# Decode attention with a gated MLP: TensorE's work on a quad of heads becomes a hardware loop, with semaphores set by hand

## The chip, the cores and the metric

The kernel runs on one core of a Trainium2 chip. The time is the device time of one execution, in microseconds (us). Its parts run side by side on that core's engines: TensorE (PE, with its weight loads listed apart as PEld), VectorE (DVE), ScalarE (ACT), GpSimd (POOL) and SyncE (SP). SP computes nothing here; it issues the large transfers from device memory to SBUF. An engine takes its instructions in program order, and a wait holds back all that stands behind it on the same engine.

## The reference

One token per batch row (B = 2, model width D = 576) goes through two branches, and a gate mixes the results. All of it is float32.

```python
g = _sigmoid((x * gate_w).sum(-1, keepdims=True))
# branch A: attention with a cache; H = 32 heads, Sk = 4096 positions, Dh = 128
q = (x @ wq).reshape(B, Sq, H, Dh).transpose(0, 2, 1, 3)
scores = jnp.einsum("bhqd,bhkd->bhqk", q, k_cache) * (Dh ** -0.5)
p = _softmax(scores, axis=-1)
o = jnp.einsum("bhqk,bhkd->bhqd", p, v_cache)
a = o.transpose(0, 2, 1, 3).reshape(B, Sq, H * Dh) @ wo
# branch B: MLP with F = 4608
h = _gelu(jnp.einsum("bsd,df->bsf", x, w1) + b1)
b = jnp.einsum("bsf,fd->bsd", h, w2) + b2
return g * a + (1 - g) * b
```

Nearly all the data are the two caches: 2 x 32 x 4096 x 128 float32 each for K and for V.

## The kernel before

**Tiles.** Four heads of one batch row make a quad; there are 16 quads, i = 0 to 15. The K rows of a quad, K(i), fill one slot of SBUF: 128 partitions x 16384 float32, 8192 KB, 32 partitions to a head. So do its V rows, V(i). There are three such slots. K alternates between slots 0 and 1, and V(i) goes through slot 2, except the last: V(15) goes into slot 0, where K(14) was.

**Start.** `wq` and `w1` are loaded into the same slots, TensorE makes q (line 170, in PSUM, spread to all partitions) and the MLP's hidden row (line 186), and VectorE and ScalarE apply the activation.

**A quad**, in the loop of line 294:

- `qk(i)`: VectorE multiplies K(i) by q in place (line 230) and sums over Dh (line 231) into the scores `st`; lines 232 to 234 find the maximum of each group of 32 partitions. ScalarE takes the exponential of each head (line 237) into `p`, with the sums in `rs`.
- `av(i)`: TensorE multiplies `p` with V(i), 32 matmuls into one bank of PSUM (line 245, called the products below); ScalarE copies that bank to SBUF (line 249, `avs`).
- `combine(i)`: five small matmuls (lines 258 and 262) add `avs` and `rs` into the bank `oall`, where the results of all quads gather. In the program it stands after `qk(i + 1)`.

`p`, `avs`, `rs`, `st` and the bank of the products exist twice, and quads take turns.

**Order of the transfers.** SP issues K(i + 2) once line 231 has read K(i) out of its slot, and V(i + 1) once the products of quad i have read V(i) out of slot 2. V(15) is the exception: its slot is free when line 231 of quad 14 is done. Behind the quads come the rows of `w2` and `wo` (line 273): 28 rows of `w2` into slot 2, after the products of quad 14; 14 rows of `wo` into slot 1, after line 231 of quad 15; the other 8 rows of `w2` and the last 5 of `wo` into slot 0, after V(15) has been read.

**End.** VectorE scales the gathered outputs into `oT` (lines 323 to 331), TensorE multiplies `hg` by `w2` and `oT` by `wo` as the rows land (lines 284 and 356), and the sum goes out (line 364).

The order on every engine is that of the program text, under a framework that sets all waits from what an instruction reads and writes.

Of the kernel before, what the change touches and what calls it, by code (L numbers as in the profile page):

```python
# [1 line left out]

# [6 lines left out]
F32 = mybir.dt.float32  # L9
AF = mybir.ActivationFunctionType  # L10
ALU = mybir.AluOpType
AX = mybir.AxisListType
P = 128


@with_exitstack
def kernel(
    ctx: ExitStack,
    tc: tile.TileContext,
    x: bass.AP,  # L20
    k_cache: bass.AP,
    v_cache: bass.AP,
    wq: bass.AP,
    wo: bass.AP,
    w1: bass.AP,
    b1: bass.AP,
    w2: bass.AP,
    b2: bass.AP,
    gate_w: bass.AP,
    out: bass.AP,  # L30
):
# [6 lines left out]
    G = H // HQ  # L38
# [15 lines left out]

    cp = ctx.enter_context(tc.tile_pool(name="cp", bufs=1))
    pp = ctx.enter_context(tc.tile_pool(name="pp", bufs=1, space=bass.MemoryType.PSUM))
    ctx.enter_context(tc.manual_schedule())

    def sb(name, *shape):
        return cp.tile(list(shape), F32, tag=name, name=name)  # L60

    slots = [sb(f"slot{i}", P, SLOT) for i in range(3)]
    dma = nc.sync.dma_start
# [6 lines left out]
    nc.scalar.dma_start(xg[:B], x.rearrange("b s d -> (b s) d"))  # L70
    nc.scalar.dma_start(xg[B:B + 1], gate_w[None, :])
    nc.scalar.dma_start(b1T, b1.rearrange("(p r) -> p r", r=FR))
    nc.scalar.dma_start(b2r, b2[None, :])


    qrow = wq[:XR].rearrange("(p r) n -> p (r n)", r=NX)
    hrow1 = w1[:XR].rearrange("(p r) n -> p (r n)", r=NX)
    wqh = slots[1][:, SLOT - WQ // 2:]
    dma(slots[0], qrow)
    dma(wqh, wq[XR:].rearrange("q (e n) -> (q e) n", e=2))  # L80
    FA = 3
    dma(slots[1][:, :FA * F], hrow1[:, :FA * F])
    dma(slots[2][:, :F], hrow1[:, FA * F:])
    w1h = slots[2][:, F:F + F // 2]
    dma(w1h, w1[XR:].rearrange("q (e n) -> (q e) n", e=2))
# [3 lines left out]
    def load_quad(src, i, s):  # L89
        g, b = divmod(i, B)  # L90
        dma(slots[s], src[b, g * HQ:(g + 1) * HQ].rearrange("h (p r) d -> (h p) (r d)", p=HP))
# [3 lines left out]
    make_identity(nc, ident)  # L95
    pt = []
    for j in range(2):
        t = sb(f"p{j}", P, R * HQ + 32)
        nc.vector.memset(t, 0.0)
        pt.append(t)  # L100
    e16 = sb("e16", P, 16)
    nc.vector.tensor_reduce(e16, ident.rearrange("p (j c) -> p j c", j=4)[:, :, :16].rearrange("p j c -> p c j"),
                            AX.X, ALU.add)
    hm = sb("hm", P, HQ)
    nc.vector.tensor_reduce(hm, ident.rearrange("p (h i) -> p h i", h=HQ), AX.X, ALU.add)
    dm = sb("dm", P, DQ)
    nc.vector.tensor_reduce(dm, ident.rearrange("p (a q) -> p q a", q=DQ), AX.X, ALU.add)
    sel = sb("sel", P, 2, 4, 32)
    hsel = sb("hsel", P, 2, 32)
    nc.vector.memset(sel, 0.0)  # L110
    nc.vector.memset(hsel, 0.0)
    for gp in range(2):
        c = slice(16 * gp, 16 * gp + 16)
        for rr in range(4):
            nc.vector.tensor_copy(
                sel[:, gp, rr, c].rearrange("p (h q) -> p h q", q=DQ),
                e16[:, 4 * rr:4 * rr + 4].unsqueeze(2).to_broadcast([P, HQ, DQ]),
            )
        nc.vector.tensor_copy(
            hsel[:, gp, c].rearrange("p (h q) -> p h q", q=DQ), hm.unsqueeze(2).to_broadcast([P, HQ, DQ])  # L120
        )


    qps = [[pp.tile([P, 512], F32, tag=f"q{b}{m}", name=f"q{b}{m}") for m in range(2)] for b in range(B)]
    avp = [pp.tile([P, 512], F32, tag=f"av{j}", name=f"av{j}") for j in range(2)]
    oall = pp.tile([P, 512], F32, tag="oall", name="oall")
    misc = pp.tile([P, 512], F32, tag="misc", name="misc")
# [4 lines left out]
    nc.vector.memset(xe, 0.0)  # L132
    for e in range(2):
        nc.vector.tensor_copy(xe[:, e, e::2], xg[:, XR:])  # L134
    NC6 = NX + 2
    xps = misc[:, :4 * NC6].rearrange("p (c k) -> p c k", k=4)
    for c in range(NC6):
        src = xg[:, c:XR:NX] if c < NX else xe[:, c - NX]
        nc.tensor.transpose(xps[:, c, :B + 1], src, ident[:B + 1, :B + 1])
    xT = sb("xT", P, NC6, 32)  # L140
    nc.vector.memset(xT, 0.0)
    nc.vector.tensor_copy(xT[:, :, :B], xps[:, :, :B])
    xq = sb("xq", P, NC6, B)
    nc.vector.tensor_scalar_mul(xq, xps[:, :, :B], SCALE)
    gT = sb("gT", P, NC6)
    nc.vector.tensor_copy(gT, xps[:, :, B])
    zps = misc[:, 64:64 + B]
    for c in range(NX + 1):
        nc.tensor.matmul(zps, gT[:, c:c + 1].to_broadcast([P, P]), xT[:, c, :B], start=(c == 0), stop=(c == NX))
    gb = sb("gb", P, B)  # L150
    g1 = sb("g1", P, B)
    nc.scalar.activation(gb, zps, AF.Exp, scale=-1.0)
    nc.vector.tensor_scalar_add(gb, gb, 1.0)
    nc.vector.reciprocal(gb, gb)
    nc.vector.tensor_scalar(g1, gb, -1.0, 1.0, op0=ALU.mult, op1=ALU.add)
# [3 lines left out]
    nc.vector.memset(g1z, 0.0)  # L159
    for u in range(2):  # L160
        nc.vector.tensor_copy(g1z[:, u, 32 * u:32 * u + B], g1[0:1])
    for u in range(2):
        nc.tensor.matmul(acc, g1z[:, u], b2r[:, u * DW:(u + 1) * DW], start=(u == 0), stop=False, skip_group_check=True)  # L163


    def q_mm(c, t, m, last):
        v = t.rearrange("p (g h d) -> p g h d", h=HQ, d=DH)
        for b in range(B):
            for h in range(HQ):
                nc.tensor.matmul(  # L170
                    qps[b][m][HP * h:HP * (h + 1)], xq[:, c, b:b + 1].to_broadcast([P, HP]), v[:, :, h],
                    start=(c == 0), stop=last, skip_group_check=True,
                )

    for c in range(NX):
        for m in range(2):
            o = c * WQ + m * WQ // 2
            q_mm(c, slots[0][:, o:o + WQ // 2], m, False)
    for e in range(2):
        q_mm(NX + e, wqh, e, True)  # L180


    hps = [avp[0], avp[1], oall]

    def mlp_mm(c, t, j, m, last):
        nc.tensor.matmul(  # L186
            hps[m][32 * j:32 * j + 32, :FC], xT[:, c], t, start=(c == 0), stop=last, skip_group_check=True
        )

    for c in range(NX):  # L190
        t = slots[1][:, c * F:(c + 1) * F] if c < FA else slots[2][:, :F]
        for m in range(3):
            for j in range(4):
                o = j * FJ + m * FC
                mlp_mm(c, t[:, o:o + FC], j, m, False)
    for m in range(3):
        for j in range(4):
            e = j // 2
            o = (j % 2) * FJ + m * FC
            mlp_mm(NX + e, w1h[:, o:o + FC], j, m, True)  # L200

    for m in range(3):
        nc.scalar.copy(hr[:, m * FC:(m + 1) * FC], hps[m][:, :FC])  # L203
# [8 lines left out]
    nc.vector.tensor_mul(gt, gt, hb)  # L212
    nc.scalar.activation(gt, gt, AF.Tanh, scale=0.7978845608028654)
    nc.vector.tensor_scalar(gt, gt, 1.0, 0.5, op0=ALU.add, op1=ALU.mult)
    nc.vector.tensor_mul(gt, gt, hb)
    nc.vector.tensor_mul(hg, gt, g1.unsqueeze(1).to_broadcast([P, FR, B]))


# [174 lines left out]
```

## Time and profile before

| | |
|---|---|
| median of 3 runs | 726.17 us (726.03 to 727.52) |
| the profiled execution | 726.76 us, of which its span is 724.9 us |
| VectorE busy | 572.6 us (79%) |
| TensorE busy | 216.1 us (30%) |
| ScalarE busy | 45.7 us (6%) |
| read from device memory | 308.57 MB, 426 GB/s over the span |

The span goes from the first instruction to the last; the remaining 1.9 us of the profiled execution lie around it. In rows of a timeline the first number is the start in us from the span's start, the second the length in us; `SPq` is SP issuing a transfer, and the length there is only the issuing. A row may merge several instructions (x2). `PE ... x64` are the 32 products of one quad, since each matmul leaves two records. The number in square brackets is how long the engine stood idle before the row, with what ended it.

### The profile page before, as it was taken

Reading aid. Unit: us, or ns where it says so; the run is one execution under the profiler, and the core shown is the slowest. Engines: PE = TensorE matmul, PEld = TensorE weight load, DVE = VectorE, ACT = ScalarE, POOL = GpSimd, SP = SyncE. Lnnn points to the kernel's source line nnn. Section 1 sums busy time; section 2 is a strip of 40 time slices with the busy share of each in tenths; the row PEclk is TensorE's granted clock in tenths of the full one; section 3 lists DMA queues with packets and bytes.
Section 4 is the critical chain, followed back from the end, with each engine's and each line's share of the span. In section 5 each row is a group of like instructions: output and inputs, shape, how many; then the busy total and the mean of one; then the engine's idle time right before and its main releaser. Section 6 shows DMA issues by size and latency. Waiting matters only on the chain.

```text
span 724.9 us, 4058 instructions
## 1 busy us (share of the span) xinstructions
PE 216.1 (30%) x1784; PEld 76.2 (11%) x1784; DVE 572.6 (79%) x127; ACT 45.7 (6%) x150; POOL 0.7 (0%) x6
## 2 busy tenths in 40 slices
PE   1690005050504022140505050504132230505564
PEld 1230002010201001010101010101010010101121
DVE  2003999999999998989899898989898989899000
ACT  0000010101010101010100101010101010100000
POOL 0000000000000000000000000000000000000000
PEclk9996557575666657575757575756657575757789
DMA  9999999999999999999999999999999999999996
GB/s 406 409 461 409 452 412 413 430 438 427 438 427 441 427 438 427 438 431 434 434 434 435 430 438 430 435 434 434 430 438 427 438 428 434 430 438 431 424 413 248
DMA packets 6809, 308.83 MB, mean 426 GB/s; under 512 B 892, under 2 KB 900, under 8 KB 1416
## 3 DMA queue, kind: packets, MB, share of 16 engines
q1 hardware_dynamic: 6632, 308.55, 98.7%
q8 instruction: 14, 0.23, 0.1%
q10 hardware_dynamic: 160, 0.03, 0.0%
q14 instruction: 3, 0.02, 0.0%
HBM read 308.57 MB, written 0.00 MB: 426 GB/s over the span
## 4 chain that ended last, share of the span: by engine, by line
DVE 48%; DMA 48%; PE 3%; issue 0%; SPq 0%; ACTq 0%; DVEq 0%
DMA slot<-in_A_k_cache_dram 33%; DVE st L231 24%; DVE slot L230 24%; DMA slot<-in_A_v_cache_dram 6%; DMA slot<-in_A_wo_dram 6%; DMA slot<-in_B_b_dram 3%; PE q L170 2%; PE av L245 1%; PE misc L163 0%; SPq L273 0%; DVE mx L232 0%; PE q L356 0%; DVE mt L233 0%; DVE nm L234 0%; ACTq L70 0%
## 5 line engine op out<-in xcount | busy, mean ns | idle before, releaser
L230 DVE TENSOR_TENSOR slot<-slot,q 128x16384 f32<-128x16384 f32 x16 | 275.5, 17219 | 44.8 <-DMA slot<-in_A_k_cache_dram 44.7
L245 PE MATMUL av<-slot,p 128*32 128x512 f32 x1024 | 144.8, 729 | 454.7 <-DMA slot<-in_A_v_cache_dram 454.7
L231 DVE TENSOR_REDUCE st<-slot 128x128 f32<-128x16384 f32 x16 | 275.5, 17219 | 1.5
L245 PEld LDWEIGHTS av<-slot,p 128*32 128x32 f32 x1024 | 40.2, 131 | 546.8 <-issue 546.8
L237 ACT ACTIVATE p<-st,nm 32x128 f32<-32x128 f32 x64 | 33.0, 516 | 180.7 <-DVE nm L234 179.4
L249 ACT COPY avs<-av 128x512 f32<-128x512 f32 x16 | 9.4, 586 | 400.8 <-PE av L245 400.8
L207 DVE STREAM_TRANSPOSE slot<-slot 128x1152 f32<-128x1152 f32 x1 | 2.2, 2197 | 40.2 <-ACT slot L203 40.2
L347 DVE COPY avs<-misc 128x288 f32<-128x288 f32 x1 | 0.5, 457 | 32.8 <-PE misc L284 32.8
L258 PE MATMUL oall<-avs,sel 128*32 128x128 f32 x128 | 17.0, 276 | 12.3 <-ACT avs L249 12.3
L170 PE MATMUL q<-slot,xq 128*32 128x512 f32 x160 | 18.7, 630 | 0.0
L258 PEld LDWEIGHTS oall<-avs,sel 128*32 128x32 f32 x128 | 12.7, 109 | 26.9 <-ACT avs L249 26.9
L284 PE MATMUL misc<-slot,hg 128*2 128x288 f32 x144 | 10.5, 453 | 9.5 <-DMA slot<-in_B_w_dram 9.5
L237 ACT ACTIVATION_READ_ACCUMULATOR p<-st,nm 32x1 f32 x64 | 12.5, 196 | 0.0
L323 DVE RECIPROCAL rg<-oall 128x2 f32<-128x2 f32 x1 | 0.2, 171 | 14.8 <-PE oall L262 14.8
L284 PE MATMUL misc<-slot,oT 128*2 128x288 f32 x108 | 7.5, 406 | 6.9 <-DMA slot<-in_A_wo_dram 4.1
L186 PE MATMUL av<-slot,xT 128*32 128x384 f32 x80 | 7.3, 486 | 0.0
L170 PEld LDWEIGHTS q<-slot,xq 128*32 128x32 f32 x160 | 5.0, 117 | 13.6 <-issue 13.6
L134 DVE COPY slot<-slot 3x64 f32<-3x64 f32 x2 | 0.3, 182 | 6.4 <-DMA slot<-in_gate_w_dram 6.4
L163 PE MATMUL misc<-slot 1*128 1x288 f32 x4 | 2.3, 715 | 10.3 <-DMA slot<-in_B_b_dram 10.3
L284 PEld LDWEIGHTS misc<-slot,hg 128*2 128x2 f32 x144 | 3.6, 92 | 16.0 <-DMA slot<-in_B_w_dram 10.2
L232 DVE TENSOR_REDUCE mx<-st 128x1 f32<-128x128 f32 x16 | 4.6, 286 | 0.5
L186 PE MATMUL oall<-slot,xT 128*32 128x384 f32 x40 | 4.1, 486 | 0.0
(58 smaller groups left out, 42.4 us busy)
## 6 DMA issues: line engine op xcount, KB each, us to landing
slot<-in_B_w_dram SPq DMA_DIRECT2D x1, 8064.0 KB, 29.3
slot<-in_B_w_dram SPq DMA_DIRECT2D x1, 6912.0 KB, 41.1
slot<-in_B_w_dram SPq DMA_DIRECT2D x2, 2304.0 KB, 46.1
slot<-in_A_wo_dram SPq DMA_DIRECT2D x1, 4032.0 KB
slot<-in_A_wo_dram SPq DMA_DIRECT2D x1, 1728.0 KB
slot<-in_B_w_dram SPq DMA_DIRECT2D x1, 1152.0 KB
slot<-in_A_wo_dram SPq DMA_DIRECT2D x1, 1152.0 KB, 36.4
slot<-in_A_wo_dram SPq DMA_DIRECT2D x2, 576.0 KB, 38.9
```

The costliest lines, as they stand in the source:

```text
L163: nc.tensor.matmul(acc, g1z[:, u], b2r[:, u * DW:(u + 1) * DW], start=(u == 0), stop=False, skip_group_check=True)
L170: nc.tensor.matmul(qps[b][m][HP * h:HP * (h + 1)], xq[:, c, b:b + 1].to_broadcast([P, HP]), v[:, :, h], start=(c == 0), stop=last, skip_gr ...
L186: nc.tensor.matmul(hps[m][32 * j:32 * j + 32, :FC], xT[:, c], t, start=(c == 0), stop=last, skip_group_check=True)
L207: nc.vector.transpose(ht.rearrange("p (r i) -> p r i", i=32), hr.rearrange("p (i r) -> p r i", r=FR))
L230: nc.vector.tensor_mul(k, k, q.unsqueeze(1).to_broadcast([P, R, DH]))
L231: nc.vector.tensor_reduce(stt[i % 2], k, AX.X, ALU.add)
L232: nc.vector.tensor_reduce(mxt[i % 2], stt[i % 2], AX.X, ALU.max)
L237: nc.scalar.activation(pt[i % 2][a, h:R * HQ:HQ], stt[i % 2][a], AF.Exp, bias=nmt[i % 2][a], accum_out=rst[i % 2][a])
L245: nc.tensor.matmul(avp[i % 2][32 * j:32 * j + 32], pt[i % 2][:, 16 * t:16 * t + 32], v[:, 512 * t:512 * (t + 1)], start=(t < 4), stop=(t > ...
L249: nc.scalar.copy(avt[i % 2], avp[i % 2])
L258: nc.tensor.matmul(oall[a, b * DH:(b + 1) * DH], sel[:, gp, rr], avt[i % 2][:, rr * DH:(rr + 1) * DH], start=first and rr == 0, stop=last ...
L284: nc.tensor.matmul(acc[64 * s + 32 * u:64 * s + 32 * u + B], lhs, wrow[name, r][:, u * DW:(u + 1) * DW], start=False, stop=last, skip_grou ...
```

## The change

The whole program is written in one block in which no framework sets waits. A class `Order` records, for named pieces of data, who wrote and who read them, and puts the semaphore waits in front of an instruction. TensorE's work on quads 0 to 14 is written once, in a hardware loop that runs on TensorE alone (`nc.Fori`, lines 405 to 407), and quad 15 follows as straight code. Inside the loop four semaphores are waited on and set by hand: `exps` (the exponentials are there), `vin` (V has landed; 16 counts to a transfer), `avc` (the copy of the products is there), and towards the others `avd` (products done) and `cmb` (combine done).

Since a loop's body has fixed addresses, `p` (now `pt`), the bank of the products, `avs` and `rs` exist once, and V is counted on one semaphore for all 15 passes. The combine stands right behind the products and its copy. It no longer adds up all quads in one bank: it writes one bank (`cps`) for all 128 partitions, and ScalarE copies the 32 partitions of its quad into the SBUF tile `oS` (line 359). `st`, `nm` and the K slots still come twice. In the start, the matmuls of the second bias stand behind those of q.

```diff
+    def soft(i):
+        j = i % 2
+        o.wait("ACT", o.deps([f"nm{j}", f"st{j}"], ["pt", "rs"]))
         for h in range(HQ):
             a = slice(HP * h, HP * (h + 1))
-            nc.scalar.activation(
-                pt[i % 2][a, h:R * HQ:HQ], stt[i % 2][a], AF.Exp, bias=nmt[i % 2][a], accum_out=rst[i % 2][a]
-            )
...
+            ins = nc.scalar.activation(pt[a, h:R * HQ:HQ], stt[j][a], AF.Exp, bias=nmt[j][a], accum_out=rs[a])
+        ins.then_inc(exps, 1)
+
+    def gather(i):
...
+        nc.scalar.wait_ge(avd, i + 1)
+        nc.scalar.copy(avs, avp).then_inc(avc, 1)
+        a = slice(32 * (g // 2), 32 * (g // 2) + 32)
+        nc.scalar.wait_ge(cmb, i + 1)
+
+        op("ACT", lambda e: e.copy(oS[a, b, g % 2], cps[a, :DH + 1]), r=[f"st{j}", f"nm{j}"], w=[f"oS{i}"])
+
+    def quad_products(e, v):
+        e.wait_ge(exps, 1).then_inc(exps, -1)
+        e.wait_ge(vin, 16).then_inc(vin, -16)
         for t in range(NT):
             j = t % 4
...
+            ins = e.matmul(avp[32 * j:32 * j + 32], pt[:, 16 * t:16 * t + 32], v[:, 512 * t:512 * (t + 1)],
+                           start=(t < 4), stop=(t >= NT - 4))
+        ins.then_inc(avd, 1)
+        e.wait_ge(avc, 1).then_inc(avc, -1)
         for rr in range(4):
...
+            e.matmul(cps[:, :DH], sel[:, rr], avs[:, rr * DH:(rr + 1) * DH],
+                     start=(rr == 0), stop=(rr == 3), skip_group_check=True)
+        e.matmul(cps[:, DH:DH + 1], hsel, rs, start=False, stop=True, skip_group_check=True).then_inc(cmb, 1)
...
     for i in range(NQ):
-        qk(i, i % 2)
+        qk(i)
         if i < NQ - 2:
-            load_quad(k_cache, i + 2, i % 2)
-        elif i == NQ - 2:
-            load_quad(v_cache, N1, i % 2)
-        else:
-            load_rows("wo", 0, WA // 2, N1 % 2, 0)
-        if i > 0:
-            combine(i - 1)
-        av(i, 2 if i < N1 else (NQ - 2) % 2)
-        if i < NQ - 2:
-            load_quad(v_cache, i + 1, 2)
-        elif i == NQ - 2:
-            load_rows("w2", 0, WA, 2, 0)
-    load_rows("w2", WA, FR, 0, 0)
+            k_load(i + 2)
+        soft(i)
+        if i < N1:
+            gather(i)
+            nc.sync.wait_ge(avd, i + 1)
+            if i < NQ - 2:
+                nc.sync.dma_start(slots[2], quad(v_cache, i + 1)).then_inc(vin, 16)
+            else:
+
+                o.wait("SP", o.deps([], ["s0"]))
+                nc.sync.dma_start(slots[0], quad(v_cache, N1)).then_inc(vin, 16)
+    o.wait("PE", o.deps(["sel0", "sel1", "sel2", "sel3", "hsel", "pt"], ["avp", "cps"]))
+    with nc.Fori(0, N1, engines=[PE], head_slot={PE: 0}):
+        quad_products(nc.tensor, slots[2])
+    quad_products(nc.tensor, slots[0])
+    gather(N1)
...
+    load_rows("w2", 0, WA, 2, 0)
+    load_rows("wo", 0, WA // 2, 1, 0, extra=o.deps([], ["s1"]))
+    load_rows("w2", WA, FR, 0, 0, extra=[done(avd, NQ)])
```

On SP, around the last V, before the change (names: `slot0` to `slot2` with a buffer number; the waits in brackets are on transfers, `DMAHW`, and on engines):

```order
L91 DMA slot2_65<-in_A_v_cache_dram 128x16384 [waits DMAHW3_49,PE_49]
L91 DMA slot1_64<-in_A_k_cache_dram 128x16384 [waits DMAHW2_49,DVE_49]
L91 DMA slot2_65<-in_A_v_cache_dram 128x16384 [waits DMAHW5_49,PE_49]
L91 DMA slot0_63<-in_A_v_cache_dram 128x16384 [waits DMAHW4_49,DVE_49]
L273 DMA slot2_65<-in_B_w2_dram 128x16128 [waits DMAHW7_49,PE_49]
L273 DMA slot1_64<-in_A_wo_dram 128x8064 [waits DMAHW6_49,DVE_49]
L273 DMA slot0_63<-in_B_w2_dram 128x4608 [waits DMAHW0_49,PE_49]
```

The same place with the change (`cDVE` counts VectorE's instructions, `avd` the quads whose products are done):

```order
L400 DMA slot2<-in_A_v_cache_dram 128x16384 [waits avd]
L82 DMA slot1<-in_A_k_cache_dram 128x16384 [waits cDVE]
L400 DMA slot2<-in_A_v_cache_dram 128x16384 [waits avd]
L404 DMA slot0<-in_A_v_cache_dram 128x16384 [waits cDVE,avd]
L82 UNCONDITIONAL_BRANCH
L82 DMA slot2<-in_B_w2_dram 128x16128
L82 DMA slot1<-in_A_wo_dram 128x8064 [waits cDVE]
L82 DMA slot0<-in_B_w2_dram 128x4608 [waits avd]
```

The order of the transfers is the same. The row that fills slot 0 with V(15) waited on VectorE alone beside an old transfer, and now waits on `avd` as well, at the value 15; the `w2` row behind it has no wait left.

On TensorE, two quads before the change:

```order
L245 MATMUL av0_109<-slot2_65,p0_81 32x512 [waits DMAHW7_49,Activation_49]
L245 MATMUL av0_109<-slot2_65,p0_81 32x512 x31
L258 MATMUL oall_111<-avs0_310,sel_91 32x128 [waits Activation_49]
L258 MATMUL oall_111<-avs0_310,sel_91 32x128 x3
L262 MATMUL oall_111<-rs0_308,hsel_92 32x1
L245 MATMUL av1_110<-slot2_65,p1_83 32x512 [waits DMAHW1_49,Activation_49]
L245 MATMUL av1_110<-slot2_65,p1_83 32x512 x31
```

The loop with the change, and the first row of quad 15 behind it:

```order
L406 ISA [waits cACT,cDVE]
L406 UNCONDITIONAL_BRANCH
L366 MATMUL bank4<-slot2,pt 32x512 [waits exps,vin]
L366 MATMUL bank4<-slot2,pt 32x512 x31
L371 MATMUL bank5<-avs,sel 128x128 [waits avc]
L371 MATMUL bank5<-avs,sel 128x128 x3
L373 MATMUL bank5<-rs,hsel 128x1
L406 REGISTER_ALU
L406 COMPARE_AND_BRANCH
L366 MATMUL bank4<-slot0,pt 32x512 [waits exps,vin]
```

The products and the combine of a quad stand in the same order as before; what is new between two quads is a register operation and a branch, and the combine's outputs are 128 partitions high where they were 32.

More of the change, by code (lines that the diff above doesn't have):

```diff
@@ L32, with kernel, body @@
+def kernel(tc, *args):
+    with tc.tile_critical():
+        body(tc, *args)
+def body(tc, x, k_cache, v_cache, wq, wo, w1, b1, w2, b2, gate_w, out):
     nc = tc.nc
@@ L173, in q_mm @@
                 )
[L175 to L191, printed above, removed]
+        return ins
```

475 lines of the change are left out of this document (276 added, 199 removed).

## Prediction

> **What bounds the kernel now.** I read the slices of the span first, then the bytes, then three stretches of 39 us.
>
> ```profile
> span 724.9 us, 4058 instructions
> DMA  9999999999999999999999999999999999999996
> HBM read 308.57 MB, written 0.00 MB: 426 GB/s over the span
> 607.00:646.00 39.00, 10.57 (x74) 3.56 (x74) 35.41 (x6) 2.65 (x9) 0.00 (x0) 0.63 1.00 434
> 646.00:685.00 39.00, 20.56 (x148) 7.13 (x148) 23.91 (x8) 3.24 (x10) 0.00 (x0) 0.72 1.00 431
> 685.00:724.00 39.00, 20.05 (x300) 7.11 (x300) 1.72 (x6) 0.00 (x0) 0.00 (x0) 0.91 0.81 344
> ```
>
> In a stretch's row the last three numbers are the TensorE clock, the busy share of the DMA engines and GB/s. The DMA engines are full from the start to the last slice, at 434 GB/s in the steady part; VectorE is busy 35.41 of 39 us, TensorE 10.57. The time is 308.57 MB / 434 GB/s = 711 us, and 14 us of start and end. So one question decides about any edit: does it ever leave the DMA engines without a transfer? For that I read the timeline of the last quads.
>
> ```profile
> 614.88 9.48 PE L245 MATMUL av<-slot,p 128*32 128x512 f32 x64 [28.50 <-DMA slot<-in_A_v_cache_dram]
> 624.42 5.89 SPq L91 DMA_DIRECT2D slot<-in_A_v_cache_dram  x2
> 624.48 0.59 ACT L249 COPY avs<-av 128x512 f32<-128x512 f32 x1 [30.19 <-PE av L245]
> 625.12 1.06 PE L258 MATMUL oall<-avs,sel 128*32 128x128 f32 x8 [0.76 <-ACT avs L249]
> 626.01 0.20 PE L262 MATMUL oall<-rs,hsel 128*32 128x1 f32 x2
> 629.99 0.28 DVE L232 TENSOR_REDUCE mx<-st 128x1 f32<-128x128 f32 x1
> 632.79 0.19 ACT L237 ACTIVATION_READ_ACCUMULATOR p<-st,nm 32x1 f32 x1
> 634.12 17.22 DVE L230 TENSOR_TENSOR slot<-slot,q 128x16384 f32<-128x16384 f32 x1 [3.38 <-DMA slot<-in_A_k_cache_dram]
> 653.58 8.90 PE L245 MATMUL av<-slot,p 128*32 128x512 f32 x64 [27.37 <-DMA slot<-in_A_v_cache_dram]
> 662.54 0.33 SPq L273 DMA_DIRECT2D slot<-in_B_w_dram  x1
> 668.69 0.33 SPq L273 DMA_DIRECT2D slot<-in_A_wo_dram  x1
> 672.94 9.46 PE L245 MATMUL av<-slot,p 128*32 128x512 f32 x64 [8.60 <-DMA slot<-in_A_v_cache_dram]
> 678.12 0.33 SPq L273 DMA_DIRECT2D slot<-in_B_w_dram  x1
> 685.65 0.23 DVE L331 TENSOR_TENSOR oT<-avs,rg 128x64 f32<-128x64 f32 x1
> 691.90 8.41 PE L284 MATMUL misc<-slot,hg 128*2 128x288 f32 x112 [7.65 <-DMA slot<-in_B_w_dram]
> ```
>
> Each row that ends with "<-DMA" dates a landing. K(15) lands at 634.1, V(14) at 653.6, V(15) at 672.9, 28 rows of `w2` at 691.9: 19.4 us apart, back to back. The SP row x2 holds two issues: V(14) at 624.42, when the products of quad 13 end (614.88 + 9.48), and V(15) at about 630.0, when line 231 of quad 14 ends (line 232 follows at 629.99). So V(15) is queued 23.6 us before V(14) has landed. The chain of waits says the same, and that the end hangs on the queue:
>
> ```profile
> 629.98 42.83 DMA slot<-in_A_v_cache_dram
> 680.39 39.87 DMA slot<-in_A_wo_dram
> ...
> 721.01 0.47 PE q L356 x8
> ```
>
> The last piece waits for the last row of `wo`, which lands just before 721.0.
>
> **The change part by part.** *V(15) waits for the products of quad 14: the term that decides.* In the order after the change this transfer waits on `avd` at 15. Those products cannot begin before V(14) has landed, at 653.58, and they end at 662.48. At 653.58 nothing else is queued: the `w2` row stands behind V(15) on SP, and the `wo` row needs line 231 of quad 15 (it went out at 668.69) and stands behind both. The DMA engines run dry. V(15) goes out at 662.54, where the `w2` row went out before (0.06 us behind the products), and starts on an empty queue. How long does an 8192 KB transfer take then? The trace has one, the first transfer of all, of the same shape:
>
> ```profile
> 0.74 0.39 SPq L79 DMA_DIRECT2D slot<-in_A_wq_dram  x1
> slot<-in_A_wq_dram SPq DMA_DIRECT2D x1, 22.1
> ```
>
> It takes 22.1 us from issue to landing, 2.7 more than the 19.4 of one that follows another. V(15) lands at 662.54 + 22.1 = 684.6, where it landed at 629.98 + 42.83 = 672.8: **11.8 us later**. Bounds: with no start-up at all, 662.54 + 19.4 = 681.9, +9.1. Dearest in the trace is a transfer that was issued into a queue about to run dry:
>
> ```profile
> 105.26 0.33 SPq L91 DMA_DIRECT2D slot<-in_A_k_cache_dram  x1
> 109.50 9.58 PE L245 MATMUL av<-slot,p 128*32 128x512 f32 x64 [54.63 <-DMA slot<-in_A_v_cache_dram]
> 148.94 8.64 PE L245 MATMUL av<-slot,p 128*32 128x512 f32 x64 [28.06 <-DMA slot<-in_A_v_cache_dram]
> ```
>
> K(2) goes out at 105.26 and V(1) lands behind it at 148.94, so K(2) at 148.94 - 19.4 = 129.5, 24.3 after its issue; part of that was V(0)'s remainder (landed at 109.50), hence an upper bound: +14.0. I take 22.1, since that transfer also met an empty queue. [...]
>
> *What follows V(15).* The products of quad 15 move from 672.9 to about 684.7 and end at 694. The second part of `w2` waits for them now; before, it went out at 678.12. In the queue then are `w2` (till 691.9 + 11.8 = 703.7) and 14 rows of `wo`, so 9.7 us remain and nothing runs dry again. `oT` was ready at 685.9, 3.5 us after the products; with one more copy of 0.6 us that is about 698, and it is wanted only behind the `w2` rows. So the whole tail moves rigidly, and no later slack takes the 11.8 back: the end waits for arriving rows up to the last.
>
> *The other V loads.* They waited for the products before as well, so nothing is added: V(14) went out at 624.42, with K(15) under way until 634.1, 9.7 us ahead; less the 2.7 of start-up, 7.0 us of cover. Without it each us would cost one us in 14 quads.
>
> *The loop's branch, and waits on TensorE.* They stand between 626.2, where the combine ends, and the next landing; TensorE sits idle 27.4 us there. Cost 0. A few sequencer steps ahead of the first product (two waits instead of one) I put at 0, with 0.2 us as the bound.
>
> *Single `p`, `rs`, `avs`.* The exponentials of quad i + 1 now wait until ScalarE has copied the combine of quad i, because the copy stands ahead of them on ScalarE. That is done at 626.2 + 0.6 (an `avs` copy takes 0.59); line 232 of the next quad starts only at 629.99, the exponentials were ready at 633.0, and the products want them at 653.6. Cost 0, cover 20.6 us. VectorE's next write of the same `st` waits for that copy too; it is line 231 of quad 15, behind line 230 that ends at 651.3. Cost 0. The combine's outputs (1.06 us and 0.20 now) become four times as high, inside the same gap.
>
> *Start and end.* The q matmuls no longer stand behind the second bias, so K(0) may go out earlier; it took 28.82 us from its issue, 6.7 over the 22.1 on an empty queue, so it stood queued behind `w1`: gain 0. The block adds a meeting of the engines before the first transfer and one after the last. The rows for both, K(0) first, then the two meetings that the trace shows:
>
> ```profile
> 41.84 28.82 DMA slot<-in_A_k_cache_dram
> ...
> SPq L379 <- PEq L379: 0.7, 1, 0.7
> SPq L388 <- PEq L388: 0.6, 2, 0.4
> ```
>
> Nothing covers the meetings: bounds 0 and 0.7 + 0.6 = 1.3; I take 0.6. Less code is fetched:
>
> ```profile
> PE 216.1 (30%) x1784; PEld 76.2 (11%) x1784; DVE 572.6 (79%) x127; ACT 45.7 (6%) x150; POOL 0.7 (0%) x6
> ...
> q8 instruction: 14, 0.23, 0.1%
> ```
>
> At most 0.23 MB / 434 GB/s = 0.5 us is to be had there. I take 0.
>
> **Sum:** 11.8 + 0.6 = +12.4 us. The profiled execution would go from 726.76 (span 724.9) to 739.2, the median of 726.17, 0.6 below it, to **738.6**. Own range: 726.0 + 9.1 = 735.1 to 727.5 + 14.0 + 1.3 = 742.8.
>
> **Rivals.** *1. The loop stalls within a pass.* If TensorE had to fetch the loop's code again while the products run, each set of products would grow; from 7.0 us on, V(i + 1) comes late and each further us costs 14 us, and a smaller stall of s us still adds s once, through quad 14. A stall of 3 us gives 741.6, one of 10 us 738.6 + 10 + 3.0 x 14 = 791. For it: the branch is new. Against it: the 14 fetches of 0.23 MB are 16 KB each, and the body is 37 matmuls of the 892 that the program had (1784 records), so it needs no new piece of code in mid-pass unless it lies across a boundary; a fetch at the branch has 27 us. [...]
>
> *2. The transfers catch up: not slower.* Here the queue empties as I say, but what is left then, V(15) with 8.39 MB, `w2` with 10.62 and `wo` with 9.44 (from their shapes), runs faster than before. Short stretches do show more:
>
> ```profile
> 25.00:30.00 5.00, 5.00 (x24) 1.47 (x26) 0.00 (x0) 0.00 (x0) 0.00 (x0) 1.00 0.82 354
> 30.00:35.00 5.00, 5.00 (x52) 1.44 (x48) 0.00 (x0) 0.00 (x0) 0.00 (x0) 1.00 1.17 509
> ```
>
> From 653.6 to the last landing near 721.0 these 28.45 MB take 67.4 us; at 509 GB/s it would be 55.9. That gives 738.6 - 11.5 = 727.1, no change, and it decides from about 500 GB/s. Against it: the neighbour of 509 is 354, and the stretches of 39 us quoted at the start lie at 434 and 431; the peaks are large packets ending in one stretch or the next.
>
> *3. The meetings of the block cost more*, with code to fetch on the way, 3 to 6 us in all instead of 0.6: 741 to 744. It is the same sign, and only the first transfer's start and the rows after the last output tell it.
>
> **How the numbers follow.** My forecast 0.84, rival 1 0.06 (a third of it under 742.8), rival 3 0.05, rival 2 0.05. A difference of 0.2% (1.5 us) is about what a measurement of this kernel can tell from none. The first, second and third of these are slower, 0.95; of rival 2's 0.05 I give 0.03 to no change and 0.02 to faster. The range is the own range, 735.1 to 742.8: it leaves out rival 2, most of rival 1 and half of rival 3, with the edges of the forecast.
>
> **What would show it.** In the profile after: the slices of DMA show a dent near 650 to 665 and nowhere else; V(15) is issued when the products of quad 14 end, and lands 31 us after V(14) instead of 19.4; all rows behind them are 11 to 13 us later, all before 650 within 1 us of their places; the first transfer goes out at 0.7 to 1.5 us. Wrong: products in the loop that last over 10.5 us, landings of V more than 39 us apart in the steady part (rival 1), the last 28.4 MB in under 60 us (rival 2), or a first transfer after 2 us (rival 3).

## The result, and the profile after

The changed kernel takes 738.49 us (median of 6, 737.96 to 739.19) against 726.21 us (median of 6, 725.24 to 727.52) before: a ratio of 1.0167, 95% interval 1.0154 to 1.0180. It is slower by 12.3 us. The forecast was 738.6.

The page of the changed kernel, its span and its slices:

```profile
span 737.4 us, 4073 instructions
...
DMA  9999999999999999999999999999999999939995
GB/s 399 412 443 445 416 419 430 434 434 434 434 431 434 437 434 430 434 437 430 434 430 441 434 430 430 437 430 437 430 437 430 434 430 434 437 153 402 445 415 227
```

One slice stands out: the 36th, 645 to 664 us, with 153 GB/s; the same slice before had 438. The stretches of 12 us around it (the last two numbers: busy share of the DMA engines, GB/s) and the timeline of TensorE and SP show what happens there:

```profile
640.00:652.00 12.00, 0.00 (x0) 0.00 (x0) 11.96 (x2) 0.00 (x0) 0.00 (x0) 0.50 0.77 333
652.00:664.00 12.00, 10.09 (x74) 3.68 (x74) 12.00 (x1) 0.85 (x2) 0.00 (x0) 0.84 0.26 87
664.00:676.00 12.00, 0.00 (x0) 0.00 (x0) 3.93 (x4) 2.06 (x8) 0.00 (x0) 0.59 1.01 437
```

```profile
652.23 8.85 PE L366 MATMUL bank<-slot,pt 128*32 128x512 f32 x64 [27.24 <-PEq L363]
661.13 0.33 SPq L404 DMA_DIRECT2D slot<-in_A_v_cache_dram  x1
661.50 0.43 SPq L82 DMA_DIRECT2D slot<-in_B_w_dram  x1
683.21 8.72 PE L366 MATMUL bank<-slot,pt 128*32 128x512 f32 x64 [20.10 <-PEq L363]
703.24 8.83 PE L454 MATMUL bank<-slot,hg 128*2 128x288 f32 x112 [9.28 <-DMA slot<-in_B_w_dram]
```

V(14) lands at 652.2. Its products run until 661.1, and V(15) is issued 0.05 us later. It lands at 683.2: 22.1 us after its issue, and 31.0 us after V(14). Before, that distance was 19.4 us (653.58 to 672.94). Meanwhile the DMA engines moved 87 GB/s over 12 us. The wait named beside the products is now TensorE's own sequencer (`PEq`), which holds the wait for `vin` (the count that says that V has landed); it is still the landing of V that ends it (the last of the 16 counts of V(15) came at 683.08 us, its products began at 683.21).

The rest of the difference is small, and of both signs. V(14) itself lands 1.4 us earlier than before. The second part of `w2` lands 10.3 us later than before, and yet the output goes out 12.1 us later. The rows for both and for the last rows of `wo`, in the kernel before and then in the change:

```profile
708.51 2.12 PE L284 MATMUL misc<-slot,hg 128*2 128x288 f32 x32 [1.87 <-DMA slot<-in_B_w_dram]
715.46 1.15 PE L284 MATMUL misc<-slot,oT 128*2 128x288 f32 x16 [1.16 <-DMA slot<-in_A_wo_dram]
717.55 1.14 PE L284 MATMUL misc<-slot,oT 128*2 128x288 f32 x12 [0.94 <-DMA slot<-in_A_wo_dram]
721.88 0.65 SPq L364 DMA_DIRECT2D out_dram<-avs  x1
```

```profile
718.80 2.12 PE L454 MATMUL bank<-slot,hg 128*2 128x288 f32 x32 [2.43 <-DMA slot<-in_B_w_dram]
725.74 4.20 PE L454 MATMUL bank<-slot,oT 128*2 128x288 f32 x28 [0.80 <-DMA slot<-in_A_wo_dram]
733.96 0.65 SPq L82 DMA_DIRECT2D out_dram<-pt  x1
```

The TensorE clock of the change in two stretches there (third number from the end):

```profile
721.00:724.00 3.00, 1.04 (x20) 0.49 (x24) 0.00 (x0) 0.00 (x0) 0.00 (x0) 1.00 1.00 422
724.00:727.00 3.00, 2.20 (x24) 0.44 (x20) 0.00 (x0) 0.00 (x0) 0.00 (x0) 0.52 1.00 411
```

28 records (the rows of 16 and 12, one row now) took 1.15 + 1.14 us before, and 4.20 us now. At 724 the granted clock fell to half, just when the last rows came. Four parts make the +12.5 us of the profiled spans: -1.4 at V(14), +11.6 at V(15), +1.8 from there to the output and +0.4 from the output to the end (737.4 - 733.96 against 724.9 - 721.88).

### The profile page after: what moved, and what is told of

The parts are those of the page before. It is cut to its first block, busy times and chain, and to the rows that moved or that the text cites. A ratio compares the mean times of both kernels' runs of the same rounds, so it can differ in the third digit from the quotient of the medians.

```text
span 737.4 us, 4073 instructions
## 1 busy us (share of the span) xinstructions
PE 223.6 (30%) x1784; PEld 79.8 (11%) x1784; DVE 572.7 (78%) x123; ACT 49.6 (7%) x166; POOL 0.7 (0%) x6
## 5 line engine op out<-in xcount | busy, mean ns | idle before, releaser
L336 DVE TENSOR_TENSOR slot<-slot,bank 128x16384 f32<-128x16384 f32 x16 | 275.5, 17218 | 44.9 <-DMA slot<-in_A_k_cache_dram 44.9
L366 PE MATMUL bank<-slot,pt 128*32 128x512 f32 x1024 | 146.1, 735 | 461.4 <-PEq L363 461.4
L366 PEld LDWEIGHTS bank<-slot,pt 128*32 128x32 f32 x1024 | 40.3, 132 | 554.7 <-issue 554.7
L347 ACT ACTIVATE pt<-st,nm 32x128 f32<-32x128 f32 x64 | 33.0, 516 | 153.3 <-DVE nm L340 152.5
L235 PE MATMUL bank<-slot,xq 128*32 128x512 f32 x160 | 19.7, 656 | 8.1 <-DMA slot<-in_A_wq_dram 8.1
L371 PE MATMUL bank<-avs,sel 128*128 128x128 f32 x128 | 18.1, 284 | 12.7 <-PEq L369 12.7
L371 PEld LDWEIGHTS bank<-avs,sel 128*128 128x128 f32 x128 | 15.5, 191 | 26.8 <-issue 26.8
L454 PE MATMUL bank<-slot,hg 128*2 128x288 f32 x144 | 11.0, 466 | 11.7 <-DMA slot<-in_B_w_dram 11.7
L347 ACT ACTIVATION_READ_ACCUMULATOR pt<-st,nm 32x1 f32 x64 | 12.5, 196 | 0.0
L454 PE MATMUL bank<-slot,oT 128*2 128x288 f32 x108 | 9.7, 489 | 3.6 <-DMA slot<-in_A_wo_dram 3.6
L235 PEld LDWEIGHTS bank<-slot,xq 128*32 128x32 f32 x160 | 5.1, 120 | 21.9 <-issue 13.6
L454 PEld LDWEIGHTS bank<-slot,hg 128*2 128x2 f32 x144 | 3.7, 93 | 18.5 <-DMA slot<-in_B_w_dram 12.3
```

Of the source, the lines that this page charges most:

```text
L235: ins = e.matmul(qps[b][m][HP * h:HP * (h + 1)], xq[:, c, b:b + 1].to_broadcast([P, HP]), v[:, :, h], start=(c == 0), stop=last, skip_grou ...
L336: op(V, lambda e: e.tensor_mul(k, k, q.unsqueeze(1).to_broadcast([P, R, DH])), r=["q", s], w=[s])
L347: ins = nc.scalar.activation(pt[a, h:R * HQ:HQ], stt[j][a], AF.Exp, bias=nmt[j][a], accum_out=rs[a])
L366: ins = e.matmul(avp[32 * j:32 * j + 32], pt[:, 16 * t:16 * t + 32], v[:, 512 * t:512 * (t + 1)], start=(t < 4), stop=(t >= NT - 4))
L371: e.matmul(cps[:, :DH], sel[:, rr], avs[:, rr * DH:(rr + 1) * DH], start=(rr == 0), stop=(rr == 3), skip_group_check=True)
L454: ins = e.matmul(acc[64 * s + 32 * u:64 * s + 32 * u + B], lhs[:, r], wrow[name, r][0][:, u * DW:(u + 1) * DW], start=False, stop=r >= hi ...
```

## The experiments

The theory: the price is the dry queue alone, and a transfer that starts on it lands 22 us after its issue. The rivals: the loop or the single buffers cost part of it; a dry queue costs a fixed price, however long it is dry; the transfers make the loss good. The times of the kernel before beside these runs had medians of 725.95 to 726.36 us.

### The last V early, on a semaphore of its own

The wait had a reason: `vin` counts to 16 for each V, so two V loads under way would be counted as one. With a semaphore of its own the last V needs no wait for the products.

```diff
             gather(i)
-            nc.sync.wait_ge(avd, i + 1)
             if i < NQ - 2:
+                nc.sync.wait_ge(avd, i + 1)
                 nc.sync.dma_start(slots[2], quad(v_cache, i + 1)).then_inc(vin, 16)
             else:
                 o.wait("SP", o.deps([], ["s0"]))
-                nc.sync.dma_start(slots[0], quad(v_cache, N1)).then_inc(vin, 16)
+                nc.sync.dma_start(slots[0], quad(v_cache, N1)).then_inc(vlast, 16)
+                nc.sync.wait_ge(avd, i + 1)
...
-    quad_products(nc.tensor, slots[0])
+    quad_products(nc.tensor, slots[0], vlast)
```

> Edit: the last V load is counted on a semaphore of its own and goes out when line 337 of quad 14 is done, without waiting for the products of quad 14; loop, single buffers and all else stay. Theory (the dry queue is the whole cost): V(15) issued near 628.6, landing 19.4 us after V(14) instead of 31.0, time 738.5 - 11.6 = 726.9, within 1 us of the kernel before. Rival A (the loop, the single buffers or the block cost part of it): the dent in DMA is gone, but the time stays 2 us or more above the kernel before, 728.5 to 732. Rival B (the tail's half TensorE clock, 1.8 us in the profile of the change, belongs to the new program and not to the phase of the clock): the last wo products run at half clock here too, and the time is about 728.5.

Measured: 724.80 us (12 executions), 0.9984 of the kernel before (0.9975 to 0.9994). The issue of the last V, the landings of V(14) and V(15), and the stretch that had been empty:

```profile
628.36 0.33 SPq L404 DMA_DIRECT2D slot<-in_A_v_cache_dram  x1
652.02 9.24 PE L367 MATMUL bank<-slot,pt 128*32 128x512 f32 x64 [26.85 <-PEq L364]
671.37 9.80 PE L367 MATMUL bank<-slot,pt 128*32 128x512 f32 x64 [8.07 <-PEq L364]
```

```profile
652.00:664.00 12.00, 10.49 (x74) 3.77 (x74) 12.00 (x1) 0.84 (x2) 0.00 (x0) 0.81 1.01 437
```

V(15) follows V(14) by 19.35 us and the queue stays full. The whole loss is gone with this one wait, so neither the loop nor the single buffers cost anything that can be seen; rival A falls. The sign of rival B is there, but not its time: in this execution too the last rows met half the clock (0.52 from 715 to 718 us), and 12 records took 2.08 us where 1.14 is usual.

```profile
714.41 2.08 PE L455 MATMUL bank<-slot,oT 128*2 128x288 f32 x12 [0.96 <-DMA slot<-in_A_wo_dram]
```

What I had not expected is that the variant is faster than the kernel before, by 1.5 us, and 13.7 us faster than the change, 1 to 2 us more than the dry queue explains.

### The same wait in the kernel before

```diff
-        elif i == NQ - 2:
-            load_quad(v_cache, N1, i % 2)
...
-        av(i, 2 if i < N1 else (NQ - 2) % 2)
+        av(i, 2)
...
         elif i == NQ - 2:
-            load_rows("w2", 0, WA, 2, 0)
-    load_rows("w2", WA, FR, 0, 0)
+            load_quad(v_cache, N1, 2)
+            load_rows("w2", 0, WA, 0, 0)
+    load_rows("w2", WA, FR, 2, 0)
...
```

> Edit on the kernel before: V(15) goes into slot 2 behind V(14), so that it waits for the products of quad 14, and the rows that stood in slot 2 behind it go into slot 0, in the same order; no loop, double buffers as before. Theory: the same dry queue, V(15) lands 31 us after V(14), time 726.2 + 11.7 = 737.9 (737 to 739). Rival A: less than that, by what the loop and the single buffers cost in the change (2 to 6 us less).

Measured: 739.06 us (4 executions, 737.43 to 739.27), ratio 1.0174 (1.0160 to 1.0189), at the upper edge of what was expected.

```profile
653.17 8.49 PE L245 MATMUL av<-slot,p 128*32 128x512 f32 x64 [27.77 <-DMA slot<-in_A_v_cache_dram]
661.72 0.33 SPq L91 DMA_DIRECT2D slot<-in_A_v_cache_dram  x1
683.58 8.65 PE L245 MATMUL av<-slot,p 128*32 128x512 f32 x64 [20.07 <-DMA slot<-in_A_v_cache_dram]
```

The same wait, put into the kernel before with its double buffers and without a loop, costs as much as the whole change: the landing comes 21.9 us after the issue, 30.4 us after V(14).

### How long it is dry: part of the products, and twice

Two variants of the change let V(15) go after the first, or after the sixteenth, of the 32 matmuls; by then the count of V(14) has been taken off `vin`.

```diff
             ins = e.matmul(avp[32 * j:32 * j + 32], pt[:, 16 * t:16 * t + 32], v[:, 512 * t:512 * (t + 1)],
                            start=(t < 4), stop=(t >= NT - 4))
+            if t == 0:          # the other variant: t == 15
+                ins.then_inc(vread, 1)
...
-            nc.sync.wait_ge(avd, i + 1)
             if i < NQ - 2:
+                nc.sync.wait_ge(avd, i + 1)
...
                 o.wait("SP", o.deps([], ["s0"]))
+                nc.sync.wait_ge(vread, i + 1)
                 nc.sync.dma_start(slots[0], quad(v_cache, N1)).then_inc(vin, 16)
+                nc.sync.wait_ge(avd, i + 1)
```

> Edit on the change: V(15) waits only until the first product of quad 14 has been issued and done (V(14) has landed and been counted), not until the last. Theory (time = issue of V(15) + 22.1 us): V(15) is issued about 0.6 to 1.1 us after V(14) lands instead of 8.9, lands about 23 us after it instead of 31.0, and the time is 738.5 - 8 = 730.5 (729.5 to 731.5). A rival by which the dry queue has a fixed price however long it lasts: 736 or more. A rival by which the start-up costs nothing: 727.5.

> Edit on the change: V(15) waits for the first 16 of the 32 matmuls of quad 14, not for all of them. Theory (landing = issue + 22 us): the first half runs at half clock, V(15) is issued 5.5 to 7 us after V(14) lands instead of 8.9 to 9.5, lands 27.5 to 29 us after it, and the time is 735 to 737. Rival (a fixed price): 738.5.

A third lets the `w2` load behind V(15) wait for the products of quad 15, which it need not:

```diff
-    load_rows("w2", 0, WA, 2, 0)
+    load_rows("w2", 0, WA, 2, 0, extra=[done(avd, NQ)])
```

> Edit on the change: the w2 load behind V(15) waits for the products of quad 15 too, though its slot is free, so the queue runs dry a second time. Theory (landing = end of the products + 22 us for about 8 MB): w2 goes out near 692.0, lands near 713.8 instead of 703.2, and the time is 738.5 + 10.6 = 749.1 (748 to 750.5). Rival (a dry stretch is made good in part by the later transfers): under 747.

Issue of V(15) and its landing, in the variant of the first matmul, then in the variant of the sixteenth:

```profile
653.71 0.33 SPq L407 DMA_DIRECT2D slot<-in_A_v_cache_dram  x1
675.79 9.45 PE L367 MATMUL bank<-slot,pt 128*32 128x512 f32 x64 [12.49 <-PEq L364]
```

```profile
658.53 0.33 SPq L407 DMA_DIRECT2D slot<-in_A_v_cache_dram  x1
680.48 8.88 PE L367 MATMUL bank<-slot,pt 128*32 128x512 f32 x64 [16.60 <-PEq L364]
```

In the variant with the second wait, V(15) and then `w2` (the first `wo` rows, which stand behind `w2` on SP and went out at 667.27 in the change, go out at 694.54 here):

```profile
663.03 0.33 SPq L404 DMA_DIRECT2D slot<-in_A_v_cache_dram  x1
684.90 9.21 PE L366 MATMUL bank<-slot,pt 128*32 128x512 f32 x64 [19.89 <-PEq L363]
694.17 0.33 SPq L82 DMA_DIRECT2D slot<-in_B_w_dram  x1
716.45 8.69 PE L454 MATMUL bank<-slot,hg 128*2 128x288 f32 x112 [20.30 <-DMA slot<-in_B_w_dram]
```

| V(15) waits for | issued after V(14) landed | lands after its issue | lands after V(14) | time, median and range, us |
|---|---|---|---|---|
| nothing (own semaphore) | 23.7 before it | | 19.4 | 724.80 (724.22 to 727.69) |
| the first matmul | 2.0 | 22.1 | 24.1 | 731.36 (729.64 to 732.38) |
| the sixteenth | 5.8 | 22.0 | 27.7 | 734.96 (733.90 to 735.22) |
| all (the change) | 8.9 | 22.1 | 31.0 | 738.49 (737.96 to 739.19) |
| all, and `w2` for the products of quad 15 | 9.7 | 21.9, `w2` 22.3 | 31.6 | 750.28 (749.29 to 750.77) |

From the first matmul to the change the issue moves by 6.9 us and the time by 7.1. From the own semaphore to the first matmul the landing moves by 4.7 us; the profiled executions differ by as much (729.64 - 724.76 = 4.9), the medians by 6.6, and the rest is not explained. So, to within some 2 us, there is no fixed price beyond the 2.7 us of start-up (22.1 - 19.4), and nothing is made good later. The expectations held but for edges: the half clock did not last for the whole first half with the sixteenth (it was 0.50 from 640 to 652 us and 0.80 on the mean from 652 to 664, so by an estimate half until about 656.8, 4.1 of the 5.8 us; in the change 0.50 until 655.8 and 1.00 from 655.9 to 661.1), the first matmul's count reached SP 2.0 us after the landing where I had put 0.6 to 1.1, the time with the sixteenth lies just under the 735 expected, and the second dry stretch cost 11.8 us instead of 10.6, since the products of both quads took longer than in the change (V(15) was issued 0.8 us later after V(14), and the products of quad 15 took 9.2 us) and `w2` landed 0.3 us later.

### The loop written out

```diff
-    with nc.Fori(0, N1, engines=[PE], head_slot={PE: 0}):
-        quad_products(nc.tensor, slots[2])
+    for _ in range(N1):
+        quad_products(nc.tensor, slots[2])
```

In the change:

> Edit on the change: the loop over 15 quads is written out as straight code, with the same semaphores and single buffers. Theory: the branch lies in TensorE's idle time of 27 us, so 738.5, within 1 us of the change. Rival A (the branch costs): 2 us or more under the change. Code fetched rises from 0.10 MB towards 0.23 MB, worth 0.3 us at most.

And in the variant with the own semaphore:

> Edit on the variant with its own semaphore for the last V (724.8 us, 1.5 under the kernel before): the loop is written out as straight code. Theory C (the 1.5 us come from the code that TensorE no longer fetches, 6 fetches instead of 14, which hold up the cache loads): V(0) to V(14) lands over about 544 us as in the kernel before (544.1) and not 542.5, and the time is 726.0 to 726.4. Rival (they come from the semaphores by hand, the order of the start, or the end): the time stays at 724.8, within 0.5.

Measured: in the change 738.67 us (4 executions, 738.40 to 739.29), no difference; with the own semaphore 726.18 us (12 executions), 1.0004 of the kernel before (0.9993 to 1.0015), where the loop gave 0.9984 (0.9975 to 0.9994). So the branch costs nothing that can be measured, and the 1.5 us by which the variant beat the kernel before are gone when the loop is. The meetings of the block, the semaphores by hand and the order of the start then come to nothing that can be told, within an interval of -0.5 to +1.1 us. The code fetched is 14 pieces (0.23 MB) straight and 6 (0.10 MB) with the loop:

```profile
q8 instruction: 6, 0.10, 0.1%
```

V(0) lands at the same time in both kernels; it was 109.50 us before, and in the change:

```profile
109.48 8.86 PE L366 MATMUL bank<-slot,pt 128*32 128x512 f32 x64 [55.73 <-PEq L363]
```

From the landing of V(0) to that of V(14), the five profiles of straight code (before twice, the kernel before with the wait, the two of this section) took 543.3 to 544.1 us, mean 543.8; the eight with the loop (the change twice, the own semaphore with and without the tail below, first and sixteenth matmul, second wait, tail alone) 542.1 to 543.6, mean 542.8. Fourteen quads at 38.70 us would be 541.8. Theory C fits, but the two groups overlap, and in the change itself the loop was worth 0.2 us by the medians and not 1.4, with about a us of uncertainty on each.

The traces show which loads were late, and by which of their parts. They keep the time of each of the 16 counts by which a load reports its parts; the load has landed with the last. K(2), the load behind V(0), comes 0.2 to 2.0 us late in all thirteen profiles, with a fetch or without. Of the 27 loads from there to V(14), ten in all came more than 0.05 us late, by 0.16 to 1.53. In all ten the first count was on time to 0.06 us and only later ones were late, and in all ten a fetch of instructions had begun in the 21 us before the landing, though a run of straight code has nine fetches in this stretch and a run with the loop two. So the late parts came with a fetch in ten cases of ten; that the fetch holds them up is an inference from these ten, and the runs do not show by what means.

For the repeat of the kernel before:

> No edit: the kernel before once more, for the landings of V(0) to V(14) and the tail. Theory C expects 543.6 us or more from V(0) to V(14) again, with one or more gaps over 39 us in 14; the rival of chance expects anything from 542 up.

It took 726.36 us, and 543.8 us from V(0) to V(14), with one gap of 40.4 us (to V(1)), one of 39.0 (to V(6), 38.95) and the rest at 38.7. That is what theory C expected, though not far from the highest run with a loop (543.6).

### More code on an idle engine

A price for each fetch can be tried the other way round, with more code in the variant with the own semaphore:

```diff
+    scr = nc.alloc_sbuf_tensor("scr", [1, 2560], mybir.dt.uint8).ap()
+    for n in range(2560):
+        nc.gpsimd.memset(scr[:, n:n + 1], 0.0)
```

> Edit on the variant with its own semaphore for the last V (724.8 us): GpSimd, which has nothing to do, writes 2560 single bytes to a scratch tile at the start; 160 KB more code, 10 more fetches. Theory C (each 16 KB fetch holds up the cache loads by 0.12 to 0.18 us): 16 fetches, V(0) to V(14) over 543.8 us or more, time 726.0 to 726.6. Rival (only the bytes count, 0.16 MB at 434 GB/s = 0.4 us, or nothing): 724.8 to 725.2.

Measured: 735.38 us (4 executions, 734.93 to 735.50), ratio 1.0124 (1.0107 to 1.0140): 10.6 us for 160 KB of code on an engine that nobody waits for. Both expectations missed, by far. The slices, the fetches, the first work on K(0), and three stretches:

```profile
DMA  9999988999999999999999999999999999999994
...
q14 instruction: 22, 0.18, 0.1%
```

```profile
78.76 17.22 DVE L340 TENSOR_TENSOR slot<-slot,bank 128x16384 f32<-128x16384 f32 x1 [14.44 <-DMA slot<-in_A_k_cache_dram]
```

```profile
0.00:50.00 50.00, 26.08 (x220) 9.93 (x224) 4.34 (x25) 1.46 (x2) 41.46 (x1212) 1.00 0.99 419
50.00:100.00 50.00, 7.25 (x88) 2.27 (x78) 24.98 (x10) 1.50 (x4) 39.64 (x1188) 0.63 1.00 428
100.00:200.00 100.00, 22.88 (x156) 7.92 (x160) 99.62 (x15) 7.93 (x28) 5.59 (x168) 0.60 0.94 403
```

K(0) has landed at 78.8 instead of 70.7, and V(0) at 121.5 instead of 109.5, while GpSimd writes (until about 109 us); from V(1) on the quads are 38.7 to 38.9 us apart again. VectorE's instructions took their 17.22 us. Until 100 us the DMA engines moved as many bytes as without the extra code (419 and 428 GB/s, against 420 and 424 there); only the landings came late.

The 16 counts of these loads show why. Fifteen counts of K(0) came at 68.8 to 70.8 us, as all sixteen did without the extra code (69.0 to 70.7), and the last one alone at 78.7. Of V(0), fifteen came by 109.4 and the last at 121.4. So one of the 16 parts came 7.9 and then 12.0 us behind the others. K(2) has to wait until VectorE has read K(0); it goes out at 113.3 us instead of 105.2, and from 100 to 120 us the DMA engines move only 283 and 289 GB/s.

It is the mark of the ten late loads in the runs above, each with a fetch shortly before and nothing else added, which speaks for the fetches. Whether they are all of it is not shown: the 20 added pieces, of 8 KB each, took 0.31 to 0.43 us apiece, 6.3 us together, and the late part trails by 8 and then 12 us; the fetches and the writes of the instructions fetched were not tried apart. What is shown is that 0.12 to 0.18 us for each 16 KB fetched is no constant: here it would be 1.06. GpSimd itself stood idle for 0.4 to 1.8 us before each run of 128 writes (8 KB of code; 3.65 us before the last run). One of these rows:

```profile
20.48 4.27 POOL L164 MEMSET scr<- 1x1 uint8 x128 [0.68 <-issue]
```

### The clock in the tail

```diff
+    def warm(n):
+        for _ in range(n):
+            nc.tensor.matmul(bank[0][:, :256], sel[:, 0], avs[:, :256], start=True, stop=True)
...
     acc_rows("wo", 0, WA // 2)
+    warm(3)
     acc_rows("w2", WA, FR)
+    warm(3)
     acc_rows("wo", WA // 2, 20)
+    warm(2)
     acc_rows("wo", 20, 24)
+    warm(1)
```

> Edit on the change: nine matmuls whose output nobody reads fill the waits for the last rows of w2 and wo. Theory B (in some executions TensorE's clock falls to half among these short waits, 1.8 us in the profile of the change): the clock stays at 1.00 from w2 to the end and the median falls by 0.3 to 1.8, to 736.7 to 738.2. Rival (the fall of the clock is an accident of that one profile, or costs nothing since the last rows land later): 738.5, within 0.3, or above it by what the added matmuls hold up.

Measured: 737.31 us (5 executions, 737.06 to 738.71), 1.2 under the change, at the edge of what the intervals tell apart (1.0141 to 1.0173 of the kernel before, against 1.0154 to 1.0180). In the profile the clock holds:

```profile
724.00:727.00 3.00, 2.70 (x28) 1.20 (x28) 0.00 (x0) 0.00 (x0) 0.00 (x0) 1.00 0.99 413
```

From the landing of V(15) to the span's end it took 52.2 us, against 54.2 in the first profile of the change.

> No edit: the change once more. V(15) lands 31.0 to 31.5 us after V(14) again. If the fall of TensorE's clock in the tail belongs to the program, from the landing of V(15) to the span's end it takes 54 us again; if it is the phase of the clock, anything from 51.5 to 54.5.

The change once more took 737.86 us, with 32.0 us from V(14) to V(15) (the products of quad 14 took 10.0 us) and 52.1 us from there to the end. The `w2` rows of this execution, and of the repeat of the kernel before:

```profile
719.24 3.81 PE L454 MATMUL bank<-slot,hg 128*2 128x288 f32 x32 [2.01 <-DMA slot<-in_B_w_dram]
```

```profile
708.17 3.81 PE L284 MATMUL misc<-slot,hg 128*2 128x288 f32 x32 [2.24 <-DMA slot<-in_B_w_dram]
```

Both took 3.81 us where 2.12 is usual: here the fall came earlier, where the wait for the next rows still hid it (0.34 and 0.20 us of that wait were left, of 2.03 without a fall). So it belongs neither to the last rows nor to the change; its place differs from execution to execution, and a fall that meets the last rows is the one that costs time. Of the twelve profiles without the added matmuls, nine show such a fall between the `w2` rows and the output and three show none (the kernel before, the same with the late V, the loop written out in the change). The two profiles with them show none. As 52.1 us for the tail were reached here without the added matmuls, the 52.2 above cannot be credited to them alone. V(15) came later than expected (32.0 us, not 31.0 to 31.5).

Both edits together:

> Both edits together on the change: the own semaphore for the last V, and the nine matmuls in the waits of the tail. If their effects add (-13.7 and -1.2 us): 738.5 - 14.9 = 723.6, about 1.2 under the variant with the own semaphore alone (724.8) and 2.7 under the kernel before. Rival (with the queue full the tail waits for its rows and not for the clock): 724.8, within 0.5.

Measured: 724.96 us (11 executions, 724.18 to 725.84), 0.9985 of the kernel before (0.9976 to 0.9994): no better than the own semaphore alone. The sum of 723.6 missed and its rival held. The highest of its executions is 725.8 instead of 727.7, no more than that. Between the two kernels with the filled tail the wait costs 737.31 - 724.96 = 12.4 us.

## Why the prediction was right, point by point

**The term that decides held: 11.6 us in the profiled execution against 11.8.** The prediction put V(15)'s issue at the end of the products of quad 14 and its landing 22.1 us later. Measured: issue 0.05 us behind the products, landing 22.1 us later, 31.0 us after V(14), against 31.06 by the prediction's numbers; in the repeat 32.0, with longer products (10.0 us), which makes it 12.6. The nine loads of about 8 MB that met an empty queue late in these runs landed 21.8 to 22.3 us after their issue. So the choice of the first transfer of all as the price was right, and the two bounds, none and 24.3, were too wide.

**"The whole tail moves rigidly"** held for the transfers (V(15) and the second part of `w2` both 10.3 us later in spans whose V(14) lands 1.4 us earlier), not quite for TensorE: a fall of its clock that met the last rows added 1.8 us in the profiled execution. The prediction had no term for it. Two of its signs came out beyond their bounds for the same reasons: K(15) landed 1.3 us earlier than before, where it allowed 1, and V(15) came 10.3 us later, where it said 11 to 13. With the tail filled the wait is worth 12.4 us, without it 13.7; the difference of 1.3 us may be what the falling clock costs in the median, though each of the two is uncertain by about a us.

**"Less code", 0**, is the term that was mis-sized, and "start and end", +0.6 us, a little. The first transfer went out 0.2 us later (0.95 instead of 0.74), but K(0) landed at 70.7 in both kernels; the end grew by 0.4. As a whole, the block in the written-out variant with its own semaphore gives 726.18 against 726.36, which tells neither 0.6 nor nothing. With the loop's shorter code V(14) landed 1.4 us earlier in the first profile of the change; by the medians the loop was worth 1.4 in one pair of kernels and 0.2 in another. The prediction allowed at most 0.5, from the bytes over the rate of all engines, and took none. That was the wrong measure by what the runs showed: ten loads came 0.16 to 1.53 us late by the last of their 16 counts, each with a fetch in the 21 us before, and the 160 KB of added code, 0.4 us by the same measure, cost 10.6 us. This error and the missing clock term have opposite signs and nearly cancel, so that 738.6 lies so close to 738.49 is in part luck. The first transfer of the change:

```profile
0.95 0.86 SPq L82 DMA_DIRECT2D slot<-in_A_wq_dram  x2
```

**Costs put at nothing** held: the loop's branch (738.67 written out), the single buffers (the variant with the own semaphore has them all and no loss), the other V loads (V still lands every 38.7 us in the change, from V(1) on).

**The rivals.** A stall within a pass would have shown products over 10.5 us; they took 8.35 to 10.02, and 8.36 to 9.76 before; and over the fifteen passes of the loop the change's trace has two fetches, of 8 KB each, at 216.5 and 217.1 us. Transfers that catch up were excluded by the series above, in which each us of a later issue cost a us (the issue moved by 6.9 us, the time by 7.1). The prediction's two short stretches of 354 and 509 GB/s lie at 434.1 and 434.2 when the packets under way at their edges (55,296 bytes, 2.04 us each) are shared out by time. Dearer meetings of the block would have sent the first transfer out after 2 us; it went at 0.95, and the end grew by 0.4.

## What to carry to other kernels

When the DMA engines are the bound, read a change by its issues alone: for each transfer, what is queued when its new wait can first be over. A wait that only protects a count (two loads on one semaphore) is mended with a second semaphore; here that turned a loss of 12.3 us into a gain of 1.5 (which goes with the loop's shorter code, since it is gone when the loop is written out), and at 724.8 us it beats both kernels. A forecast that hits can hide errors that cancel, so it pays to undo the main term alone and look at what is left. And a load has landed only with the last of its parts: something small can cost more than its bytes, as 160 KB of added code did here (10.6 us, with the last of K(0)'s 16 counts 8 us behind the others).

## What the runs showed of the hardware

- A transfer of 8 MB that meets an empty queue lands 21.8 to 22.3 us after its issue, one behind another 19.35 us after it. By the difference (22.1 - 19.4), an estimate, a transfer has to be issued at least 2.7 us before the queue is empty. The nearest row says that more is safer: K(2) goes out 4 us before V(0) lands, and still comes 0.2 to 2.0 us late.
- TensorE's granted clock fell to half (1.00 to 0.50) between the `w2` rows and the output, where work comes in short pieces with waits of 0.8 to 2.6 us, at changing places (724 us in one execution of the change, 719 in the next), in nine of twelve profiles; in the two with nine idle matmuls in the waits it did not.
- Ten loads came 0.16 to 1.53 us late with their first part on time, and each had a fetch of instructions begun in the 21 us before it landed; that the fetch was the cause is inferred from that. With 160 KB of extra code on GpSimd one of the 16 parts of K(0) came 8 us behind the others and the kernel took 10.6 us longer, though that is 0.05% of the bytes. GpSimd stood idle for 0.4 to 1.8 us before nearly every 8 KB of it. How much of the 10.6 us the fetches did, and how much the instructions, stays open.
